# Seven half-size products for eight in the first layer of the last token block

## The chip, the cores and the metric

The kernel is one program on one core of a Trainium2 chip. The core's engines are named here as its profile names them: PE (TensorE, matrix products), with PEld for its weight loads; DVE (VectorE); ACT (ScalarE); POOL (GpSimd); SP (SyncE), which only issues transfers. Each engine takes its instructions in the order in which the program issued them to it, and instructions on different engines wait for each other through semaphores. The metric is the device time of one execution, in microseconds; before the change it was 321.52 us, the median of three runs (321.17 to 321.62).

## The reference

Two stages are chained. The first is a retention layer without softmax: for 8 batches and 8 heads of 576 positions with 64 columns, the scores q k^T / 8 are multiplied by a lower-triangular decay matrix gamma_h^(i-j), and then by v. Its output, as 4608 tokens of 512 columns, is the `x` of the second stage, a bilinear feed-forward layer with 1536 hidden columns:

```python
def _moe_ref(x, w_a, w_b, w_out):
    a = x @ w_a
    b = x @ w_b
    return (a * b @ w_out).astype(np.float32)
```

`a`, `b` and their product are here called the first layer (512 to 1536, twice), and the product with `w_out` the second (1536 to 512). The product of `a` and `b`, transposed, is `hT`: hidden columns on the partitions, tokens along the free axis.

## The kernel before

The 4608 tokens go through the feed-forward part in blocks: 512, 256, 256, and seven more of 512. In text and code they are counted by pairs of 256 tokens, `n` from 0 to 17 (`NP` is 18), so that the last block holds the pairs 16 and 17. The retention work of later tokens is threaded in between the products of earlier blocks. `ffn_block` is a generator that issues a few matrix products and yields their cost in units of one product of 512 columns; a list `todo` of (due time, function) pairs, written by hand, is worked off at those yields that are marked as an edge (in the first layer: after each hidden group's second half). A second list, `jobs`, holds small vector operations with a priority and a cost; `work(budget)` issues those that fit. The scheduler is manual: the order in which the Python code issues instructions is the order on each engine.

**First layer** (`ffn_block`, up to L1164). The 1536 hidden columns are 12 groups `F` of 128. For each group four products (one per 128 rows of `w_a`, 512 tokens wide) make `pa` in one PSUM bank, ACT copies it to `ha` in bfloat16 (L1152), four products make `pb` (L1159), and DVE multiplies `ha` by `pb` into `hT[:, F]` (L1164). `pa` and `pb` take turns in the four banks of the pool `ps_ffn` (tag `ab`); a bank is taken again when its reader is done, in the order in which banks came free.

**Second layer** (`rows_mixed`, L975 on). For the last six blocks it works on pairs of hidden groups (`p` from 0 to 5, groups `2p` and `2p+1`) and replaces eight products of half width by seven on sums of operands. The sums of weights (`wo_sums`) are made once. The sums of `hT` are made for each block by `row_sums` (L944): five additions or subtractions on DVE, three into `hsum` and two in place in `hT`. They are issued as jobs, for the pairs 0 to 3 together after group 7 and for the pairs 4 and 5 together after group 11. In the last block (`closing`), the products come in this order: ways 3 and 4 on `hT` as it is, way 1 on a sum, ways 5 and 2 on the two sums made in place, then 7 and 6 on sums. `lessen` and `add_last` (L1055, L1062) put the results together on DVE, and POOL adds two kept copies (L1045); the outputs of the block before last are stored from the list `formed`, in the last block.

The helper pools that matter below: `straight`, `crossed` and `less` (two buffers each, float32 copies of 128 x 512), `ps_sc` (two banks) and `ps_o` (one buffer of two banks), `stage` (the buffers of incoming q, k and v) and `nat`.

Of the kernel before, what the change touches and what calls it, by code (L numbers as in the profile page):

```python
# [18 lines left out]
def kernel(  # L19
# [10 lines left out]
    nc = tc.nc  # L30
# [4 lines left out]
    NTOK = B * S  # L35
    NC = DM // 128
# [8 lines left out]
    NP = NTOK // 256  # L45
# [34 lines left out]
    stage = pool("stage", 3)  # L80
    nat = pool("nat", 3)
# [5 lines left out]
    ha_pool = pool("ha", 6)  # L87
    o_pool = pool("osb", 4)
    late, early = {}, ExitStack()
# [13 lines left out]
    ps_ffn = pool("ps_ffn", 4, PS)  # L103
    opening, ps_sc, ps_o = ExitStack(), {}, {}
# [17 lines left out]
    wa_sb = big.tile([128, NC, DFF], BF16)  # L122
    wb_sb = big.tile([128, NC, DFF], BF16)
# [18 lines left out]
    shared = {}  # L142
# [117 lines left out]
    def pair_tables(step):  # L260
# [6 lines left out]
        else:  # L267
            for h in (2 * step - 2, 2 * step - 1):
# [660 lines left out]
    WIDE = DM // 2  # L929
# [11 lines left out]
        out = wo_sums[:, step // 3, p0:p0 + 2]  # L941
        nc.vector.tensor_tensor(out, one, other, op=op)

    def row_sums(hT, sums, p0, p1):  # L944

        even, odd = (hT[:, 2 * p0:2 * p1].rearrange(
            "p (f e) (g k s) -> p e k f g s", e=2, g=2, k=2)[:, e]
            for e in (0, 1))
        a11, a21, a12, a22 = even[:, 0], even[:, 1], odd[:, 0], odd[:, 1]
        to = [sums[:, i, p0:p1] for i in range(3)]  # L950
        return [(1, (p1 - p0) / 8 + 0.2,
                 lambda e=e: nc.vector.tensor_tensor(*e[:3], op=e[3]))  # L952
                for e in ((to[0], a11, a22, ALU.add),
                          (to[2], a12, a22, ALU.subtract),
                          (to[1], a21, a11, ALU.subtract),
                          (a12, a11, a12, ALU.add),
                          (a21, a21, a22, ALU.add))]

    def store_mixed(G, osb, cols=slice(0, 2 * DM), on=nc.sync):

# [17 lines left out]
    def store_formed():  # L978
        while formed:
            store_mixed(*formed.pop(0))  # L980

    def rows_mixed(tok0, hT, sums):
# [3 lines left out]
        pair = [tok0 // 256 + g for g in (0, 1)]  # L986
# [50 lines left out]
        crossed, lesses = {}, {}  # L1037
# [13 lines left out]
        def lessen(g):  # L1051
            lesses[g] = late["less"].tile([128, 2, WIDE], FP32, tag="less",
                                          name="less")
            for ks in (slice(0, 1), slice(1, 2)) if closing else (slice(0, 2),):
                nc.vector.tensor_tensor(  # L1055
                    lesses[g][:, ks],
                    both[g].unsqueeze(1).to_broadcast(
                        [128, ks.stop - ks.start, WIDE]),
                    crossed[g][:, ks], op=ALU.subtract)
# [33 lines left out]
        first, rest = range(NP2 - 1), (NP2 - 1,)  # L1093
# [19 lines left out]
        yield 0, True  # L1113

    def ffn_block(tb, tok0, n, runs):

        xT = x_of(tok0, n)
        hT = h_pool.tile([128, NF, 512], BF16, tag="h", name="hT")
        if tok0 >= 256 * MIXED:
            pools_mixed()  # L1120
            sums = late["hsum"].tile([128, 3, NF // 2, 2, 128], BF16, tag="hsum",
                                  name="hsum")
        f0 = 0
        for count in runs:
            has = {}
            if tb == 0 and f0 == 0:
                for c in range(2, NC):
                    for F in range(count):
                        begin_with(F, c, 1)
            for F in range(f0, f0 + count):  # L1130
                fs = slice(F * 128, (F + 1) * 128)
                pa = (begun[F] if tb == 0 and F in begun else
                      ps_ffn.tile([128, 512], FP32, tag="ab", name="pa"))
                for c in range(NC):
                    if tb == 0 and (F, 0, 0) in begun:
                        if (F, c, 1) not in begun:
                            begin_with(F, c, 1)
                        if c < NC - 1:
                            yield n / 512, False
                        continue  # L1140
                    nc.tensor.matmul(pa[:, 0:n], wa_sb[:, c, fs],  # L1141
                                     xT[:, c],
                                     start=(c == 0), stop=(c == NC - 1))
                    if c < NC - 1:
                        yield n / 512, False
                if n == 512 and tb:
                    pop()
                pass_on(1)
                if F == 2:
                    store_formed()  # L1150
                ha = ha_pool.tile([128, 512], BF16, tag="ha", name="ha")
                nc.scalar.copy(ha[:, 0:n], pa[:, 0:n])  # L1152
                has[F] = ha
                yield n / 512, False
            for F in range(f0, f0 + count):
                fs = slice(F * 128, (F + 1) * 128)
                pb = ps_ffn.tile([128, 512], FP32, tag="ab", name="pb")
                for c in range(NC):
                    nc.tensor.matmul(pb[:, 0:n], wb_sb[:, c, fs],  # L1159
                                     xT[:, c],  # L1160
                                     start=(c == 0), stop=(c == NC - 1))
# [12 lines left out]
                yield n / 512, True  # L1174
            f0 += count
        if tb == 0:
            yield from rows_together(tok0, hT, (0, 1))
        if tok0 >= 256 * MIXED:
            yield from rows_mixed(tok0, hT, sums)
            return  # L1180
        for u in range(2 if tb == 0 else 0, n // 128):
            osb = half_of(o_pool, u, [DM], FP32, "osb")
            po = ps_ffn.tile([128, 512], FP32, tag="ab", name="po")
            for F in range(NF):
                nc.tensor.matmul(po, hT[:, F, u * 128:(u + 1) * 128],  # L1185
                                 wo_sb[:, F],
                                 start=(F == 0), stop=(F == NF - 1))
# [12 lines left out]
            yield 1, True  # L1200
# [99 lines left out]
    starts, at = {}, 0.0  # L1300
# [84 lines left out]
        casts[n], turns[n] = placed[n] - 96, placed[n] - 58  # L1385
    for fn, places in ((ahead, casts), (turn, turns)):
        todo += [(at, fn, (n,)) for n, at in places.items()]
    todo.sort(key=lambda e: e[0])

    at = 0.0  # L1390
    tok = 0
    for tb, n in enumerate(blocks):
        runs = WCOLS if tb == 0 else [1] * NF
        for cost, edge in ffn_block(tb, tok, n, runs):
            at += cost
            while todo and edge and at >= todo[0][0]:
                _, fn, args = todo.pop(0)
# [33 lines left out]
```

## Time and profile before

| | |
|---|---|
| median of three runs | 321.52 us (321.17 to 321.62) |
| the profiled execution: its time / its span | 320.63 us / 318.4 us |
| PE busy | 308.0 us, 97% of the span |
| DVE / POOL / ACT busy | 198.9 / 155.6 / 145.7 us |
| last block, first layer (284.4 to 305.1 us) | PE 20.59, DVE 10.81, ACT 7.02, POOL 0.00 us busy of 20.70 |
| last block, second layer (305.1 to 314.5 us) | PE 9.38, DVE 5.55, ACT 2.40, POOL 2.51 us busy of 9.40 |
| from the last product to the end (314.5 to 318.4 us) | PE 0, DMA share 0.51 |

Times inside the execution are counted from the start of its span. In the lines of the timeline the columns are: start, length, engine, source line, operation, output <- inputs, shapes, number of instructions merged into the line, and in brackets the idle time before it with what ended it. The length of a merged line runs from its first start to its last end; a product's end is modelled and overlaps the next product, so the pace of products is read from start to start. In the lines of the groups, the numbers after the bar are busy time in total, mean ns of one, and the idle time before them.

### The profile page before, as it was taken

The numbers are of one execution on the slowest core, as the hardware profiler recorded it, in microseconds if no ns is written. First come the engines' busy times: TensorE is split into PE (matmuls) and PEld (weight loads), VectorE is DVE, ScalarE is ACT, GpSimd is POOL, SyncE is SP. The second block draws the span as 40 slices with busy tenths as digits, with TensorE's granted clock in tenths as the row PEclk, the third lists the DMA queues.
The fourth block names the chain that finished last, engine by engine and source line by source line (L and its number), as shares of the span: only waits on it lengthen the run. The fifth ranks groups of instructions, "written<-read, shape, count | busy, mean of one in ns | idle before, by whom it ended". The sixth has DMA issues, their size and how long they took to land.

```text
span 318.4 us, 9134 instructions
## 1 busy us (share of the span) xinstructions
PE 308.0 (97%) x3763; PEld 183.4 (58%) x3799; DVE 198.9 (62%) x376; ACT 145.7 (46%) x324; POOL 155.6 (49%) x169
## 2 busy tenths in 40 slices
PE   7899999999999999999999999999999999999995
PEld 3554457768544554448654864477446744674474
DVE  5745346867757563479658854776567656834563
ACT  7745346536435463454454534544434443423330
POOL 3990078664986577564796089506960300030003
PEclk9999999999999999999999999999999999999999
DMA  8999999999999999999999998974430110012004
GB/s 215 255 203 207 255 231 184 193 207 182 207 178 214 229 218 179 240 193 223 241 280 201 179 229 181 198 164 129 108 68 2 76 61 0 2 74 60 0 1 132
DMA packets 144793, 50.92 MB, mean 160 GB/s; under 512 B 126576, under 2 KB 141680, under 8 KB 144752
## 3 DMA queue, kind: packets, MB, share of 16 engines
q1 hardware_dynamic: 138272, 45.10, 70.9%
q0 software_dynamic: 5808, 4.72, 9.4%
q8 instruction: 29, 0.48, 0.6%
q10 hardware_dynamic: 672, 0.52, 0.5%
q14 instruction: 12, 0.10, 0.1%
HBM read 37.75 MB, written 9.44 MB: 148 GB/s over the span
## 4 chain that ended last, share of the span: by engine, by line
PE 90%; DVE 3%; DMA 2%; issue 2%; POOL 1%; SPq 1%; ACT 0%; DVEq 0%; POOLq 0%
PE pb L1159 29%; PE pa L1141 28%; PE m L1022 16%; PE po L1185 8%; DMA vf<-in_v_dram 2%; PE po L913 2%; PE sc L703 1%; PE o L731 1%; PE o L744 1%; SPq L175 1%; PE kv L632 1%; DVE hT L952 1%; POOL vb L365 1%; DVE sums L659 1%; PE pa L902 1%
## 5 line engine op out<-in xcount | busy, mean ns | idle before, releaser
L1164 DVE TENSOR_TENSOR hT<-ha,pb 128x512 bf16<-128x512 bf16 (+1 forms) x120 | 75.8, 632 | 80.4 <-PE pb L1159 68.5
L1159 PE MATMUL pb<-xT,wb_sb 128*128 128x512 bf16 (+1 forms) x478 | 111.5, 358 | 0.4
L1152 ACT CAST ha<-pa 128x512 bf16<-128x512 f32 (+1 forms) x120 | 64.9, 542 | 96.8 <-PE pa L1141 92.0
L1141 PE MATMUL pa<-xT,wa_sb 128*128 128x512 bf16 (+1 forms) x448 | 106.4, 356 | 1.9 <-issue 1.2
L1159 PEld LDWEIGHTS <-wb_sb 128*128 128x128 bf16 x480 | 46.8, 98 | 47.5 <-issue 1.9
L1141 PEld LDWEIGHTS <-wa_sb 128*128 128x128 bf16 x472 | 45.0, 98 | 43.0 <-DVE sums L659 0.2
L1045 POOL TENSOR_TENSOR osb<-crossed,straight 128x512 f32<-128x512 f32 x12 | 15.2, 1271 | 102.8 <-ACT crossed L1034 96.3
L589 POOL TENSOR_TENSOR vb<-vf,vs 128x1024 bf16<-128x1024 f32 (+1 forms) x17 | 29.6, 1743 | 4.5 <-PE pb L1159 1.7
L1022 PEld LDWEIGHTS <-hT 128*128 128x128 bf16 x288 | 28.1, 98 | 4.7 <-issue 0.3
L562 POOL TENSOR_TENSOR qkb<-qf,qs 64x1024 bf16<-64x1024 f32 x12 | 22.9, 1911 | 14.2 <-DMA qf<-in_q_dram 9.1
L1185 PE MATMUL po<-wo_sb,hT 128*128 128x512 bf16 x113 | 26.7, 379 | 0.8 <-issue 0.6
L1022 PE MATMUL m<-wo_sums,hsum 128*128 128x256 bf16 x216 | 25.7, 273 | 0.0
L567 POOL TENSOR_TENSOR qkb<-qf,qs 64x512 bf16<-64x512 f32 x24 | 24.8, 1052 | 0.7
L1022 PEld LDWEIGHTS <-hsum 128*128 128x128 bf16 x216 | 21.1, 98 | 2.4
L952 DVE TENSOR_TENSOR hsum<-hT 128x1024 bf16<-128x1024 bf16 (+1 forms) x36 | 20.3, 591 | 0.2
L578 POOL CAST qkb<-kf 64x1024 bf16<-64x1024 f32 (+1 forms) x17 | 15.9, 935 | 8.0 <-DMA kf<-in_k_dram 7.1
L712 DVE TENSOR_TENSOR sT<-sc,mask 128x512 bf16<-128x512 f32 x30 | 19.8, 680 | 0.0
L659 DVE TENSOR_TENSOR sums<-kv,sums 128x256 f32<-128x256 f32 x44 | 18.6, 422 | 1.4
L582 POOL CAST qkb<-kf 64x512 bf16<-64x512 f32 (+1 forms) x34 | 18.8, 581 | 0.9
L1185 PEld LDWEIGHTS <-hT 128*128 128x128 bf16 x120 | 11.2, 98 | 12.6
L1022 PE MATMUL m<-wo_sb,hT 128*128 128x256 bf16 x144 | 17.0, 273 | 0.1
L1022 PE MATMUL m<-wo_sums,hT 128*128 128x256 bf16 x144 | 16.9, 273 | 0.0
(111 smaller groups left out, 283.0 us busy)
## 6 DMA issues: line engine op xcount, KB each, us to landing
qf<-in_q_dram SPq DMA_DIRECT2D x32, 256.0 KB, 5.1
vf<-in_v_dram SPq DMA_DIRECT2D x32, 256.0 KB, 5.2
kf<-in_k_dram SPq DMA_DIRECT2D x31, 256.0 KB, 4.9
out_dram<-osb SPq DMA_DIRECT2D x9, 512.0 KB, 4.1
out_dram<-osb SPq DMA_DIRECT2D x22, 128.0 KB, 2.8
wo_sb<-in_moe_w_out_dram POOLq DMA_DIRECT2D x3, 512.0 KB, 16.0
out_dram<-osb SPq DMA_DIRECT2D x6, 256.0 KB, 4.2
qf<-in_q_dram SPq DMA_DIRECT2D x8, 128.0 KB, 4.2
```

The lines of the kernel that those rows point to most:

```text
L562: nc.gpsimd.tensor_tensor(per_head(qkb[0:64, Q]), per_head(t[0:64]), by[0:64].unsqueeze(2).to_broadcast([64, 2 * H, D]), op=ALU.mult)
L567: nc.gpsimd.tensor_tensor(per_head(qkb[64:128, Q])[:, 1 - r::2], per_head(t[64:128])[:, r::2], by[64:128, r::2].unsqueeze(2).to_broadcast( ...
L589: nc.gpsimd.tensor_tensor(vb[:, e].rearrange("p (h d) -> p h d", d=D), t[:, e].rearrange("p (h d) -> p h d", d=D), decay[:, at], op=ALU.mult)
L659: nc.vector.tensor_tensor(sums[:, i], own, prev, op=ALU.add)
L712: nc.vector.tensor_tensor(sT[:, on].rearrange("p c k s -> p (c k) s"), sc[on].rearrange("p c k s -> p (c k) s"), mask3.unsqueeze(1).to_bro ...
L952: lambda e=e: nc.vector.tensor_tensor(*e[:3], op=e[3]))
L1022: nc.tensor.matmul(to, rows, cols, start=(begins and p == 0), stop=True, skip_group_check=True)
L1141: nc.tensor.matmul(pa[:, 0:n], wa_sb[:, c, fs], xT[:, c], start=(c == 0), stop=(c == NC - 1))
L1152: nc.scalar.copy(ha[:, 0:n], pa[:, 0:n])
L1159: nc.tensor.matmul(pb[:, 0:n], wb_sb[:, c, fs], xT[:, c], start=(c == 0), stop=(c == NC - 1))
L1164: nc.vector.tensor_tensor(hT[:, F, 0:n], has[F][:, 0:n], pb[:, 0:n], op=ALU.mult)
L1185: nc.tensor.matmul(po, hT[:, F, u * 128:(u + 1) * 128], wo_sb[:, F], start=(F == 0), stop=(F == NF - 1))
```

## The change

Three things change, all for the last block of 512 tokens.

1. Its first layer goes through a new generator, `last_layer`. For four of the six pairs of hidden groups (`SEVENS`: 0, 1, 3, 4) the product of [2 x 128 hidden columns, 512] by [512, 512 tokens], cut in two along each axis, is made from seven products of half size instead of eight, for `w_a` and `w_b` alike (`m` is 0 and 1, side by side in one bank): 28 matrix products of 256 columns for a pair in place of 16 of 512 columns. Partial results accumulate in the banks `main` (ways 1, 6, 7, 4), `side` (5, 3) and `aside` (2). Three of them are copied out by ACT on the way (`keep`); three quarters of a pair's `hT` are made by a DVE addition of bank and copy and a POOL multiplication (`gated`), and the fourth by ACT and DVE as before. The pairs 2 and 5 keep the old way ("a" and "b" in `ORDER`).
2. The operands need sums. `combine` makes four sums of weights for a pair of hidden-group pairs and a matrix (two pairs at a time, `combos`, in buffers of `stage`): 12 instructions on POOL and 4 on DVE, due in the block before last. `combine_rows` makes four sums of `x` of the last block on DVE, issued in `rows_mixed` of the block before last, between `lessen` and `add_last`.
3. `row_sums` for the last block is issued for each pair alone: 30 DVE instructions on 256 columns in place of 5 on 1024 and 5 on 512. The first of a pair's five comes ahead of other jobs (0.9). The budget for jobs after each step of `ORDER` is `SHARE`.

```diff
-    def row_sums(hT, sums, p0, p1):
+    def row_sums(hT, sums, p0, p1, shared=0):
...
+        order = (2, 0, 1, 3, 4)
...
+        return [(0.9 if i == 2 and p1 == p0 + 1 else 1, (p1 - p0) / 8 + 0.2,
+                 lambda e=ways[i]: nc.vector.tensor_tensor(*e[:3], op=e[3]))
+                for i in order if i >= shared]
...
             lessen(g)
+        if pair[1] == NP - 3:
+            for i in range(4):
+                combine_rows(i)
...
+    def combine(p, m, i):
...
+        out, one, other, op = [(s3, a11, a21, ALU.subtract),
+                               (s1, a21, a22, ALU.add),
+                               (s2, a22, s3, ALU.subtract),
+                               (s4, a12, s2, ALU.subtract)][i]
+        (nc.vector if i == 3 else nc.gpsimd).tensor_tensor(
+            out, one, other, op=op)
...
+    def combine_rows(i):
...
+        out, one, other, op = [(t1, b12, b11, ALU.subtract),
+                               (t3, b22, b12, ALU.subtract),
+                               (t2, b11, t3, ALU.add),
+                               (t4, b21, t2, ALU.subtract)][i]
+        nc.vector.tensor_tensor(out, one, other, op=op)
...
+        def quarter(p, way):
...
+            to = st["aside" if way == 2 else
+                    "side" if way in (3, 5) else "main"]
...
+                w, x = {1: (a11, xT[:, 0:2, g0]), 2: (a12, xT[:, 2:4, g0]),
+                        3: (s4, xT[:, 2:4, g1]), 4: (a22, t4), 5: (s1, t1),
+                        6: (s2, t2), 7: (s3, t3)}[way]
+                for c in (0, 1):
+                    nc.tensor.matmul(to[:, m], w[:, c], x[:, c],
...
+        def keep(name, own):
+            t = late[name].tile([128, 2, WIDE], FP32, tag=name, name=name)
+            nc.scalar.copy(t, own)
+            return t
+
+        def gated(t, own, to):
+            nc.vector.tensor_tensor(t, own, t, op=ALU.add)
+            nc.gpsimd.tensor_tensor(to, t[:, 0], t[:, 1], op=ALU.mult)
+
+        def after(p, way):
...
+            if way == 1:
+                st["first"] = keep("straight", st["main"])
+            elif way == 5:
+                st["third"] = keep("less", st["side"])
+            elif way == 6:
+                st["second"] = keep("crossed", st["main"])
+            elif way == 2:
+                gated(st["first"], st["aside"], hT[:, F0, g0])
+            elif way == 3:
+                gated(st["second"], st["side"], hT[:, F0, g1])
+            elif way == 7:
+                gated(st["third"], st["main"], hT[:, F1, g1])
+            else:
+                ha = ha_pool.tile([128, 512], BF16, tag="ha", name="ha")
+                nc.scalar.copy(ha[:, g0], st["main"][:, 0])
+                nc.vector.tensor_tensor(hT[:, F1, g0], ha[:, g0],
+                                        st["main"][:, 1], op=ALU.mult)
...
+    ORDER = ((1, 0), (5, 0), (2, 0), (6, 0), (1, 1), (3, 0), (7, 0), (5, 1),
+             (2, 1), (6, 1), (4, 0), ("a", 4), (3, 1), (7, 1), ("b", 4),
+             ("a", 5), (4, 1), ("b", 5),
+             (1, 3), (5, 3), (2, 3), (6, 3), (1, 4), (3, 3), (7, 3), (5, 4),
+             (2, 4), (6, 4), (4, 3), ("a", 10), (3, 4), (7, 4), ("b", 10),
+             ("a", 11), (4, 4), ("b", 11))
+    SHARE = {1: 0, 5: 0, 2: 0, 6: 0.4, 3: 0, 7: 0.4, 4: 0, "a": 0.4, "b": 0.7}
...
+            if done is not None:
+                jobs.extend(row_sums(hT, sums, done, done + 1, SHARED))
+            work(SHARE[way])
+        work(math.inf, 1)
...
+        if tok0 == NTOK - 512:
+            yield from last_layer(xT, hT, sums)
+            yield from rows_mixed(tok0, hT, sums)
+            return
...
+    todo += [(starts[NP - 4] + 2 + 4.2 * i, combine,
+              (SEVENS[i // 8 * 2], i // 4 % 2, i % 4)) for i in range(16)]
```

More of the change, by code (lines that the diff above doesn't have):

```diff
@@ L950, in row_sums @@
         to = [sums[:, i, p0:p1] for i in range(3)]
[L951 to L957, printed above, removed]
+        ways = ((to[2], a12, a22, ALU.subtract),
+                (to[1], a21, a11, ALU.subtract),
+                (to[0], a11, a22, ALU.add),
+                (a12, a11, a12, ALU.add),
+                (a21, a21, a22, ALU.add))
+        order = (2, 0, 1, 3, 4)
+        for i in range(shared):
+            out, one, other, op = ways[i]
+            nc.gpsimd.tensor_tensor(out, one, other, op=op)
+        return [(0.9 if i == 2 and p1 == p0 + 1 else 1, (p1 - p0) / 8 + 0.2,
+                 lambda e=ways[i]: nc.vector.tensor_tensor(*e[:3], op=e[3]))
+                for i in order if i >= shared]
     def store_mixed(G, osb, cols=slice(0, 2 * DM), on=nc.sync):
@@ L1113, in rows_mixed, with quarter_weights @@
         yield 0, True
+    SEVENS = (0, 1, 3, 4)
+    SHARED = 0
+    combos = {}
+    def quarter_weights(m, p0, count=1):
+        w = (wa_sb, wb_sb)[m][:, :, 256 * p0:256 * (p0 + count)].rearrange(
+            "p c (q e f) -> p e c q f", e=2, f=128)
+        return [[w[:, e, c:c + 2] for c in (0, 2)] for e in (0, 1)]
+    def combine(p, m, i):
+        if (p, m) not in combos:
+            combos[p, m] = stage.tile([128, 4, 2, 2, 128], BF16,
+                                      tag=("qf", "kf")[m], name="combo")
+            combos[p + 1, m] = combos[p, m]
+        (a11, a12), (a21, a22) = quarter_weights(m, p, 2)
+        s3, s1, s2, s4 = (combos[p, m][:, k] for k in range(4))
+        out, one, other, op = [(s3, a11, a21, ALU.subtract),
[4 more added lines that the diff above has]
+            out, one, other, op=op)
@@ new lines @@
+    row_combos = []
+    def combine_rows(i):
+        if not row_combos:
+            row_combos.append(nat.tile([128, 4, 2, 256], BF16, tag="qkb",
+                                       name="rows"))
+        x = x_of(256 * (NP - 2), 512)
+        (b11, b12), (b21, b22) = [[x[:, c:c + 2, 256 * g:256 * g + 256]
+                                   for g in (0, 1)] for c in (0, 2)]
+        t1, t3, t2, t4 = (row_combos[0][:, k] for k in range(4))
+        out, one, other, op = [(t1, b12, b11, ALU.subtract),
[3 more added lines that the diff above has]
+        nc.vector.tensor_tensor(out, one, other, op=op)
@@ new lines, in layer_mixed @@
+    def layer_mixed(xT, hT):
+        t1, t3, t2, t4 = (row_combos[0][:, k] for k in range(4))
+        g0, g1 = slice(0, 256), slice(256, 512)
+        state = {}
+        def quarter(p, way):
+            if way == 1:
+                state[p] = {
+                    "main": ps_ffn.tile([128, 2, 256], FP32, tag="ab",
+                                        name="lm"),
+                    "side": ps_sc[0].tile([128, 2, 256], FP32, tag="sc",
+                                          name="ls")}
+            st = state[p]
+            if way == 2:
+                st["aside"] = ps_o[0].tile([128, 2, 2, 256], FP32, tag="o",
+                                           name="la")[:, 0]
+            to = st["aside" if way == 2 else
+                    "side" if way in (3, 5) else "main"]
+            for m in (0, 1):
+                (a11, a12), (_, a22) = (
+                    [t[:, :, 0] for t in ts] for ts in quarter_weights(m, p))
+                s3, s1, s2, s4 = (combos[p, m][:, k, :, SEVENS.index(p) % 2]
+                                  for k in range(4))
+                w, x = {1: (a11, xT[:, 0:2, g0]), 2: (a12, xT[:, 2:4, g0]),
[3 more added lines that the diff above has]
+                    nc.tensor.matmul(to[:, m], w[:, c], x[:, c],
+                                     start=(way in (1, 2, 5) and m == c == 0),
+                                     stop=True, skip_group_check=True)
+                    yield 0.5, False
+        def keep(name, own):
[6 more added lines that the diff above has]
+        def after(p, way):
+            st = state[p]
+            F0, F1 = 2 * p, 2 * p + 1
+            if way == 1:
+                st["first"] = keep("straight", st["main"])
[14 more added lines that the diff above has]
+                                        st["main"][:, 1], op=ALU.mult)
+        return quarter, after
@@ new lines, with last_layer @@
+    ORDER = ((1, 0), (5, 0), (2, 0), (6, 0), (1, 1), (3, 0), (7, 0), (5, 1),
[5 more added lines that the diff above has]
+    SHARE = {1: 0, 5: 0, 2: 0, 6: 0.4, 3: 0, 7: 0.4, 4: 0, "a": 0.4, "b": 0.7}
+    def last_layer(xT, hT, sums):
+        quarter, after = layer_mixed(xT, hT)
+        has = {}
+        for i, (way, at) in enumerate(ORDER):
+            done = None
+            if way in ("a", "b"):
+                F = at
+                p1 = ps_ffn.tile([128, 512], FP32, tag="ab", name="p" + way)
+                for c in range(NC):
+                    w = wa_sb if way == "a" else wb_sb
+                    nc.tensor.matmul(p1, w[:, c, F * 128:F * 128 + 128],
+                                     xT[:, c], start=(c == 0),
+                                     stop=(c == NC - 1))
+                    yield 1, False
+                if way == "a":
+                    has[F] = ha_pool.tile([128, 512], BF16, tag="ha",
+                                          name="ha")
+                    nc.scalar.copy(has[F], p1)
+                else:
+                    nc.vector.tensor_tensor(hT[:, F], has[F], p1, op=ALU.mult)
+                    if F % 2:
+                        done = F // 2
+            else:
+                yield from quarter(at, way)
+                after(at, way)
+                if way == 4:
+                    done = at
+            if i == 3:
+                store_formed()
+            if done is not None:
+                jobs.extend(row_sums(hT, sums, done, done + 1, SHARED))
+            work(SHARE[way])
+        work(math.inf, 1)
```

## The prediction

> **What bounds the kernel now.** I read the page's busy shares and chain first, then the windows of the last two blocks, then the timelines of PE, DVE and POOL around the last block, and last the groups of POOL and DVE by shape for prices.
>
> ```profile
> PE 308.0 (97%) x3763; PEld 183.4 (58%) x3799; DVE 198.9 (62%) x376; ACT 145.7 (46%) x324; POOL 155.6 (49%) x169
> ...
> PE 90%; DVE 3%; DMA 2%; issue 2%; POOL 1%; SPq 1%; ACT 0%; DVEq 0%; POOLq 0%
> ```
>
> PE is busy 97% of the span, and 90% of the chain that ended last is PE.
>
> ```profile
> 252.70:284.40 31.70, 31.49 (x337) 18.95 (x340) 19.68 (x38) 11.66 (x24) 2.54 (x2) 1.00 0.09 34
> 284.40:305.10 20.70, 20.59 (x96) 9.39 (x97) 10.81 (x17) 7.02 (x12) 0.00 (x0) 1.00 0.16 52
> ```
>
> Columns: stretch, length, then busy us and instructions of PE, PEld, DVE, ACT and POOL, and the granted clock. The second row is the layer that changes: PE has no gap in it, DVE is busy 52%, POOL not at all, and the clock is 1.00. So what is taken from PE here is time, as long as the other engines keep up.
>
> ```profile
> 279.18 2.78 PE L1022 MATMUL m<-wo_sb,hT 128*128 128x256 bf16 x24
> ...
> 285.29 1.03 PE L1159 MATMUL pb<-xT,wb_sb 128*128 128x512 bf16 x4
> 286.15 1.03 PE L1141 MATMUL pa<-xT,wa_sb 128*128 128x512 bf16 x4
> ...
> 305.14 2.35 PE L1022 MATMUL m<-wo_sums,hT 128*128 128x256 bf16 x20
> 307.33 0.82 PE L1022 MATMUL m<-wo_sums,hsum 128*128 128x256 bf16 x6
> ```
>
> Start to start, 92 wide products take 305.14 - 285.29 = 19.85 us, 0.2158 each; 20 half-wide ones take 307.33 - 305.14 = 2.19 us, 0.109 each (0.1092 over longer stretches). A half-wide product costs 51% of a wide one.
>
> ```profile
> 281.36 2.58 POOL L1045 TENSOR_TENSOR osb<-crossed,straight 128x512 f32<-128x512 f32 x2 [29.20 <-ACT crossed L1034]
> ...
> 282.62 0.69 DVE L1055 TENSOR_TENSOR less<-m,crossed 128x512 f32<-128x512 f32 x1 [0.62 <-ACT crossed L1034]
> 283.37 0.75 DVE L1062 TENSOR_TENSOR osb<-m,less 128x256 f32<-128x256 f32 x2
> ...
> 306.62 1.09 DVE L952 TENSOR_TENSOR hsum<-hT 128x512 bf16<-128x512 bf16 x3
> 307.63 0.75 DVE L952 TENSOR_TENSOR hT<-hT 128x512 bf16<-128x512 bf16 x2
> ```
>
> These rows give the paces of DVE: three sums of 512 in 307.63 - 306.62 = 1.01 us, 0.337 each; sums of 1024 start 0.60 apart (306.02, 306.62). The slope is 0.267 per 512, so 0.07 is fixed, and a sum of 256 comes to 0.204. That is an estimate; no row has one.
>
> ```profile
> 170.37 1.90 POOL L589 TENSOR_TENSOR vb<-vf,vs 128x1024 bf16<-128x1024 f32 x1
> ...
> 170.87 1.95 DVE L952 TENSOR_TENSOR hsum<-hT 128x1024 bf16<-128x1024 bf16 x1
> ```
>
> A DVE sum of two SBUF operands, usually 0.69, takes 1.95 when issued 0.5 us into a POOL instruction of 1.90: it ends 0.55 after POOL does (172.27, 172.82). It waits for the running POOL instruction. DVE instructions with a PSUM operand (L1164, L712) keep 0.68 to 0.69 beside the same POOL work.
>
> **The change, part by part.** Times continue those of the profiled execution.
>
> *Products.* A changed pair issues 28 half-wide products for 16 wide ones: 28 x 0.1092 = 3.06 for 16 x 0.2158 = 3.45, 0.395 less. Four pairs: **-1.58**. The bounds: the pace of L1022, or, if these products ran at 3.45/28 = 0.123, no gain at all. I take L1022's: same width, same weight size.
>
> *Sums of weights.* POOL, 12 on 512 columns. No POOL row has bfloat16 inputs; the nearest are 128x512 f32 at 1271 ns and vb 128x512 at 1086. Their operands are weights loaded long before, so POOL takes them up at 252.2, when its adds of the block before end (249.58 + 2.58), and is done by 265.3 to 267.4, ahead of the first DVE sum of that block (268.57). Cost nothing, the cover being POOL's empty queue from 252.2 to 281.36. The four on DVE take 0.34 each and may wait up to 1.27 for a running POOL instruction; the fourth of a set follows its POOL operand by an edge or more. Behind them on DVE wait the products into hT, whose banks are asked for again some 2.6 us after they were filled, against 0.27 + 0.69 for reading them. Nothing on PE; 0 to 0.3 if the wait falls into the busy stretch at 261 to 264.
>
> *Sums of x.* Four on DVE after 283.31 (282.62 + 0.69). The first waits for POOL's second add, 281.36 + 2.58 = 283.94; the second follows at 0.34; the third reads the second and the fourth the third, 0.47 each (0.41 + 0.06, as 282.62 to 283.37 shows for 0.69). They end at 285.5. Queued behind are the four `add_last`, 0.34 each: the first two end at 286.28 instead of 284.12, the others at 286.96. They free the buffers of `less`, into which (5,0) is copied by ACT: 286.33 to 286.91. Way 3 of pair 0 needs that copy; PE comes to it at 284.42 + 5 x 0.437 = 286.60 and starts at 286.97 (waits of PE on ACT ended 0.05 to 0.06 after it early in the trace: ACT qkT to PE sc at 11.37, 11.43). **+0.37**, and 0.06 more for way 7 behind a late `crossed`. Without the POOL collision, or with it doubled, 0.1 to 0.9.
>
> *Elementwise work of the layer.* Per changed pair DVE has three additions from PSUM (0.61 start to start, as L1164 before L952) and one half (0.34), four pairs 8.7; two old pairs 4 x 0.61 = 2.4; ACT three copies of 0.58 and one half; POOL three multiplications of 256. The price of the last: 722 ns (128x256 f32, L462) and 615 (128x256 from f32 into bf16, L365); 0.72 is nearest, two full float32 operands. Upper bound 1.27, the 512 row. At 0.72 the pairs' chains hold: way 6 needs way 1's copy, 0.20 + 0.58 + 0.06 after it, and comes 0.87 after; way 4 needs way 7's addition and comes at least 1.3 us after.
>
> *Sums of hT.* 30 x 0.204 = 6.1 for what took 10 (5 x 0.60 and 5 x 0.337, 4.7). `SHARE` lets 15 out before group 11's product, 7 in the first half of `ORDER` and 8 in the second. Each may wait for a running POOL multiplication, at most 0.72; I count seven such waits, 1.4 us. DVE then has 40 instructions, 15.6 us, in the 19.6 us of the layer: it keeps up, by 4 us.
>
> *The end of the layer.* PE is done at 305.14 - 1.58 + 0.43 = 304.0. Group 11's product starts on DVE at 304.27 (0.27 after, as in every group before) and the remaining 15 sums follow from 304.88. The second layer asks last for the in-place sum a12 of pair 5, the 14th: 304.88 + 14 x 0.204 + 0.05 = 307.8. PE wants it after 20 + 6 + 4 + 5 = 35 half-wide products, 304.0 + 3.82 = 307.8. Before, the same sum was there 0.9 us early (308.04 for 308.97). So the cover is gone, and what is late next is this sum: **+0.02** at 0.204. At 0.25 a sum it is 0.9, at 0.28 1.5; at a POOL multiplication of 0.8, 0.4, and at 0.9, 0.8 (DVE then falls behind). This is the forecast's weak place.
>
> *Rest.* The stores of block 7 leave a step earlier or later on SP, with 25 us to spare; no transfer is added. The tail from 314.5 on is untouched.
>
> Sum: -1.58 + 0.43 + 0.02 = -1.1, with 0 for the weights. Profiled time 320.63 - 1.1 = 319.5. That execution stands 0.9 under the median of 321.52, so I put the median at 321.52 - 1.05 = **320.5**.
>
> [...]
>
> **The rivals.**
>
> *The small sums cost their length, not their pace (slower, or even).* Lengths are 0.69 at 1024 and 0.41 at 512, so 0.28 at 256. If each waits for the one before to end (a semaphore between them would do it), 14 take 3.9 us and a12 of pair 5 is 1.5 us late: -1.1 + 1.5 = +0.4, 321.9. It decides from 0.26 on. Against it: L952 of 512 runs three in a row at its pace. For it: no row has 256 columns, and in-place sums follow sums of the same columns. [...]
>
> *POOL is the pace of the layer.* Twelve multiplications at 1.0 us or more hold `straight`, `crossed` and `less`, hold up sums, and with them DVE: at 1.0 way 4 waits and the end comes 0.8 later than before, 322.3; at 0.9 it is -0.3, 321.2. Against it: 722 ns measured; for it, the lock with DVE, which lengthened vb from 1.90 to 2.22 at 144.7.
>
> *A bank.* If the bank that "b" 5 or "b" 11 takes is the one that (4,1) or (4,4) has just filled, PE waits for ACT and DVE: 0.2 + 0.38 + 0.05 + 0.42 + 0.06, some 1.2 each: 321.7 for one, 322.7 for both. Banks are given out in the order in which they come free, and then another one is free earlier.
>
> *The weights are not hidden.* Were POOL's sums over 1.9 us each, they would run past 275 into block 7's DVE sums and their wait of up to 1.9; some +1, 322. Against it, 1086 and 1271.
>
> *No gain in the products.* At 0.123 the change is +0.1: 321.6.
>
> **How the numbers follow.** A measurement of this kernel can tell about 0.2%, 0.64 us, from no change. The forecast (320.0 to 320.9) has 0.60. Part of its end lost (a sum at 0.23 to 0.25, or POOL at 0.8 to 0.9: 320.8 to 321.4) has 0.15, a third of which is still faster by over 0.2%. The sums at their length has 0.10, half of it same and half slower; POOL as the pace 0.05, a bank 0.04, the weights 0.04, all slower; no gain in the products 0.02, same. Faster 0.65, same 0.17, slower 0.18. Range: 319.9 is the whole cut of PE with no wait; above, to leave out only the doubled bank and POOL beyond 1.0, 322.2.
>
> **What would show it.** PE's layer ends about 1.1 us earlier against its start, with one gap of 0.4 at way 3 of pair 0 and 112 half-wide products at 0.109. DVE's sums of 256 start 0.2 apart. POOL has 12 sums between 252 and 268 and 12 multiplications of about 0.72 in the last layer. In the second layer PE waits for DVE at way 5 by 0.1 or less; a wait of a microsecond there, or a PE gap before "b" 5, "b" 11 or (4,4), makes the prediction wrong, and so does any gap in block 7.

## The result and the profile after

The changed kernel takes 319.18 us (median of 6; 318.93 to 319.87), against 321.54 us (6; 321.17 to 321.62) for the kernel before on the same chip: a ratio of 0.9932, 95% interval 0.9919 to 0.9945. It is faster by 2.36 us, where 1.05 was forecast, and the time lies 0.7 us below the lower end of the range. The profiled execution of the changed kernel takes 319.40 us, span 317.7.

The page of the changed kernel, first the busy time of each engine, then the chain that ended last by engine:

```profile
PE 310.2 (98%) x3847; PEld 188.2 (59%) x3847; DVE 208.3 (66%) x412; ACT 149.1 (47%) x332; POOL 177.8 (56%) x193
...
PE 88%; DVE 5%; SPq 2%; DMA 2%; issue 1%; ACT 1%; DVEq 0%; ACTq 0%
```

PE still bounds the kernel. Its busy time only seems to grow from 308.0 us: the page of before lacks 36 of the products (3763 records), and three more traces of that kernel have 3799 and 311.4 to 311.9 us. DVE has 9.4 us more to do and POOL 22.2. The windows of the changed kernel show where (stretch, length, busy us and instructions of PE, PEld, DVE, ACT, POOL, then granted clock, DMA share, GB/s): block 7's second layer, the last block's first layer, the last block's second layer up to its final 18 products.

```profile
275.80:284.95 9.15, 9.15 (x85) 8.21 (x84) 5.30 (x12) 2.25 (x4) 2.54 (x2) 1.00 0.00 0
284.95:304.42 19.47, 19.39 (x146) 14.07 (x145) 16.98 (x41) 10.18 (x20) 8.68 (x12) 1.00 0.17 55
304.42:311.63 7.21, 7.21 (x68) 6.42 (x67) 5.37 (x21) 1.82 (x4) 1.27 (x1) 1.00 0.01 3
```

In the layer that changed DVE is now busy 16.98 of 19.47 us, 87%, where it was 52%, and PE still has hardly a gap. The timeline of PE in the changed kernel, around the only two waits and at the start of the second layer:

```profile
286.95 0.38 PE L1192 MATMUL lm<-xT,wb_sb 128*128 128x256 bf16 x2
287.41 0.60 PE L1192 MATMUL ls<-xT,combo 128*128 128x256 bf16 x4
287.90 0.60 PE L1192 MATMUL lm<-rows,combo 128*128 128x256 bf16 x4
...
304.42 2.35 PE L1027 MATMUL m<-wo_sums,hT 128*128 128x256 bf16 x20
```

Two products from 286.95 on last 0.22, so PE could have gone on at 287.17 and did at 287.41: a wait of 0.24. The four after it take 0.437, to 287.85; the next start at 287.90, 0.05 later. After that PE runs without a gap.

Three marks lead through every trace: the start of block 7's second layer, the start of the last block's second layer, and the start of its final 18 products.

| kernel | block 7's second layer | last block's second layer | between them | final 18 products | from there to the span's end |
|---|---|---|---|---|---|
| before | 275.25 | 305.14 | 29.89 | 312.35 | 6.04 |
| changed | 275.80 | 304.42 | 28.62 | 311.63 | 6.06 |

The first mark differs from one execution to the next: it lay between 275.4 and 276.0 in three more executions of before. The 0.55 is there before the sums of weights begin: the start of block 6's second layer lies 31.78 us ahead of the mark in both (243.47 and 244.02), and POOL's first sum starts at 252.67. It is counted as chance here; over all traces the mark lies between 275.2 and 276.0 in before and between 275.4 and 277.3 in the changed kernel and its variants, and no run shows whether that is chance alone. The stretch between the first two, 1.27 us shorter, is what the change did in the last block; I had forecast 1.15 for it (1.58 less 0.43). The profiled pair adds up: 320.63 - 1.27 + 0.55 (chance) + 0.02 (tail) - 0.53 (time outside the span, 2.23 before and 1.70 after) = 319.40. But the medians are 2.36 apart: the profiled execution of before stands 0.9 below its median, that of the changed kernel 0.22 above. So another microsecond had to be found in executions that these two traces don't show.

### The profile page after: what moved, and what is told of

The parts are those of the page before. It is cut to its first block, busy times and chain, and to the rows that moved or that the text cites. A ratio compares the mean times of both kernels' runs of the same rounds, so it can differ in the third digit from the quotient of the medians.

```text
span 317.7 us, 9344 instructions
## 1 busy us (share of the span) xinstructions
PE 310.2 (98%) x3847; PEld 188.2 (59%) x3847; DVE 208.3 (66%) x412; ACT 149.1 (47%) x332; POOL 177.8 (56%) x193
## 4 chain that ended last, share of the span: by engine, by line
PE 88%; DVE 5%; SPq 2%; DMA 2%; issue 1%; ACT 1%; DVEq 0%; ACTq 0%
PE pb L1320 26%; PE pa L1302 25%; PE m L1027 15%; PE po L1346 8%; PE lm L1192 2%; SPq L175 2%; DMA qf<-in_q_dram 2%; PE po L913 2%; PE sc L703 1%; PE o L744 1%; PE o L731 1%; PE kv L632 1%; DVE hT L961 1%; PE pb L1248 1%; PE pa L1248 1%
## 5 line engine op out<-in xcount | busy, mean ns | idle before, releaser
L1325 DVE TENSOR_TENSOR hT<-ha,pb 128x512 bf16<-128x512 bf16 (+1 forms) x108 | 67.6, 626 | 68.7 <-PE pb L1320 58.4
L1320 PE MATMUL pb<-xT,wb_sb 128*128 128x512 bf16 (+1 forms) x432 | 99.3, 355 | 0.1
L1302 PE MATMUL pa<-xT,wa_sb 128*128 128x512 bf16 (+1 forms) x424 | 97.6, 355 | 0.1
L1313 ACT CAST ha<-pa 128x512 bf16<-128x512 f32 (+1 forms) x108 | 58.0, 538 | 81.8 <-PE pa L1302 79.2
L1320 PEld LDWEIGHTS <-wb_sb 128*128 128x128 bf16 x432 | 42.1, 98 | 41.9 <-issue 1.9
L1302 PEld LDWEIGHTS <-wa_sb 128*128 128x128 bf16 x424 | 40.3, 98 | 37.9 <-issue 0.4
L1346 PE MATMUL po<-wo_sb,hT 128*128 128x512 bf16 x120 | 27.8, 379 | 0.0
L961 DVE TENSOR_TENSOR hsum<-hT 128x256 bf16<-128x256 bf16 (+2 forms) x48 | 22.4, 494 | 0.4
```

The source lines that it names most:

```text
L961: lambda e=ways[i]: nc.vector.tensor_tensor(*e[:3], op=e[3]))
L1302: nc.tensor.matmul(pa[:, 0:n], wa_sb[:, c, fs], xT[:, c], start=(c == 0), stop=(c == NC - 1))
L1320: nc.tensor.matmul(pb[:, 0:n], wb_sb[:, c, fs], xT[:, c], start=(c == 0), stop=(c == NC - 1))
L1325: nc.vector.tensor_tensor(hT[:, F, 0:n], has[F][:, 0:n], pb[:, 0:n], op=ALU.mult)
L1346: nc.tensor.matmul(po, hT[:, F, u * 128:(u + 1) * 128], wo_sb[:, F], start=(F == 0), stop=(F == NF - 1))
```

## The experiments

**First set: is the excess chance, and does each part do what it should?** The changed kernel again, unaltered:

> The changed kernel once more, beside the kernel before on the same chip. Theory A (all of the gain is made in the last block, where the two traces differ by 1.3 us; the rest of the 2.4 us lies between single executions): 1.0 to 1.6 us less than before. Theory B (about 1.1 us come from outside the last block, and with this program every time): 2.1 to 2.6 us less again, and the spans of the runs, or the time outside the spans, differ by more than the last block does.

Measured: 319.50 us (6 runs) against 321.38 (17), ratio 0.9943 (0.9923 to 0.9962). The stretch is 28.63. The gain of 1.88 lies between the ranges of the two theories, and its interval (1.2 to 2.5) just reaches the 1.26 of the stretch. So some 0.6 us of excess came back, and it isn't in the stretch; that it is more than chance, these runs alone do not show.

Only the sums of weights and of x, with the last block as it was before:

```
         if tok0 == NTOK - 512:
-            yield from last_layer(xT, hT, sums)
-            yield from rows_mixed(tok0, hT, sums)
-            return
+            pass
```

> The sums of weights and of x are made where the changed kernel makes them, but the last block's first layer and its row sums are done the old way (the sums are not used). Theory A: 0 to 0.4 us slower than before, the late add_last holding a bank at the start of the last block. Theory B, with the cause in what the program adds ahead of the last block: about 1 us faster than before.

The prepared sums are made and not used. Measured: 321.33 us (12 runs), ratio 1.0002 (0.9987 to 1.0018), stretch 29.92. Twenty additional instructions on POOL and DVE cost nothing that can be seen, and they give nothing either.

The sums of x ahead of the two `cross` and `lessen`:

```
         work(math.inf)
         pass_on(math.inf)
+        if pair[1] == NP - 3:
+            for i in range(4):
+                combine_rows(i)
         for g in (0, 1):
             yield from cross(g)
             lessen(g)
-        if pair[1] == NP - 3:
-            for i in range(4):
-                combine_rows(i)
```

> The changed kernel with the four sums of x issued ahead of the products 5 and 2 of the block before last, where DVE stands idle for 3.2 us and POOL has nothing, instead of behind the second lessen. The prediction's account of the start of the layer (0.43 us of waits behind late sums): the gaps of PE at way 3 and way 7 of pair 0 go, 0.4 us less than the changed kernel. Rival (those waits only move to the next late copy): no difference beyond 0.15.

Measured: 319.21 us (5 runs), ratio 0.993 (0.991 to 0.995), stretch 303.75 - 275.40 = 28.35. The timeline of PE in this kernel, at the same two places:

```profile
286.55 0.38 PE L1192 MATMUL lm<-xT,wb_sb 128*128 128x256 bf16 x2
286.77 0.60 PE L1192 MATMUL ls<-xT,combo 128*128 128x256 bf16 x4
287.22 0.60 PE L1192 MATMUL lm<-rows,combo 128*128 128x256 bf16 x4
...
303.75 2.35 PE L1027 MATMUL m<-wo_sums,hT 128*128 128x256 bf16 x20
```

Way 3 follows after 0.22 and way 7 after 0.45: both waits are gone, and with them 0.27 of the stretch, where 0.4 was expected. It is 1.54 shorter than before, against a full cut of 1.58. By its trace this is the best of the kernels, by 0.27 us; the times (319.21 and 319.50 on one chip) don't separate it from the changed kernel.

Two pairs instead of four:

```
-             (1, 3), (5, 3), (2, 3), (6, 3), (1, 4), (3, 3), (7, 3), (5, 4),
...
+             ("a", 6), ("b", 6), ("a", 7), ("b", 7), ("a", 8), ("b", 8),
+             ("a", 9), ("b", 9), ("a", 10), ("b", 10), ("a", 11), ("b", 11))
```

> The pairs 0 and 1 by seven products as in the change, the pairs 3, 4 and 5 the old way; all sums are made. Theory A: half of the cut of 1.58 less the waits of 0.43 at its start, 0.3 to 0.5 us less than before. Theory B with a fixed 1.1 us: 1.3 to 1.6 us less.

Measured: 319.77 us (6 runs), ratio 0.9954 (0.9936 to 0.9973), stretch 305.00 - 275.60 = 29.40, 0.49 less than before. The stretch went as forecast for half the change, and again the time fell by more, 1.6 us. So the excess doesn't grow with the number of pairs.

**Second set: where is the excess?** Before three more times and the changed kernel once, all traced.

> The kernel before, traced again, to see where an ordinary execution of it (321.4 us) is longer than the one that was profiled first (320.6 us). From the start of the second layer of the block before last to the start of the last block's second layer it took 29.89 us there (28.62 with the change), and 275.25 us up to that point. Theory A (what is left of the difference lies in the waits for inputs of the first 275 us, by chance of the execution): 29.9 us again, and a start of 275.2 to 277. Theory C (long runs of wide products at the end draw a lower clock, and the change breaks them up): 30.3 us or more, with a granted clock below 1.00 there.

> The kernel before once more. Theory A: 29.9 us for that stretch and a start anywhere from 275.2 to 277; theory C: 30.3 us or more with a clock below 1.00.

> The kernel before a third time. Theory A: 29.9 us for that stretch and a start anywhere from 275.2 to 277; theory C: 30.3 us or more with a clock below 1.00.

> The changed kernel traced again beside them. Theory A: 28.6 us for the stretch, and a start of 275.2 to 277 as with the kernel before. Theory C: 28.6 us and a clock of 1.00, the start no different from that of the kernel before.

Measured: before 321.15, 320.99 and 321.56 us (8 runs each), ratios 1.0, 1.0016 and 1.0016, each interval holding 1; changed 319.09 (8 runs), 0.9935 (0.9908 to 0.9961). The stretch is 29.89 in all three traces of before and 28.62 in that of the changed kernel. Theory A falls, since the starts (275.4 to 276.0 in before, 275.9 in the changed kernel) do not favour the changed kernel. Theory C falls too: the windows of the first trace have the clock at 1.00 through the stretch and beyond, up to the last product.

```profile
275.37:305.26 29.89, 29.89 (x181) 17.59 (x180) 15.78 (x29) 9.26 (x16) 2.54 (x2) 1.00 0.11 36
305.26:314.60 9.34, 9.34 (x85) 8.13 (x83) 5.56 (x14) 2.40 (x5) 2.49 (x2) 1.00 0.10 24
314.60:317.00 2.40, 0.00 (x0) 0.00 (x0) 0.42 (x1) 0.00 (x0) 0.06 (x1) 1.00 0.90 261
317.00:319.20 2.20, 0.00 (x0) 0.00 (x0) 0.00 (x0) 0.00 (x0) 0.00 (x0) 0.52 0.28 99
```

The difference is in what comes after the products. From the final 18 products to the end, two of these traces of before take 6.8 and 6.9 us (319.3 - 312.47 in the first) and one 6.1; every trace of the changed kernel and its variants above takes 6.0 to 6.1. The transfers in the stretch from 311 to 316 us, first in the profiled execution of before that the prediction read (6.04 from the final products to the end), then in the first of the three, with its final products ahead. The rows of queues give packets, MB and the share of the 16 engines; those of stores give their number, the size of each and the median us from issue to landing.

```profile
DMA packets 404, 0.79 MB, mean 159 GB/s; under 512 B 80, under 2 KB 208, under 8 KB 404
...
q1 hardware_dynamic: 336, 0.66, 48.4%
q10 hardware_dynamic: 68, 0.14, 7.3%
...
out_dram<-osb SPq DMA_DIRECT2D x6, 128.0 KB, 2.2
out_dram<-osb ACTq DMA_DIRECT2D x1, 256.0 KB, 2.3
```

```profile
312.47 2.13 PE L1022 MATMUL m<-wo_sums,hsum 128*128 128x256 bf16 x18
...
DMA packets 184, 0.53 MB, mean 107 GB/s; under 512 B 54, under 2 KB 54, under 8 KB 183
...
q1 hardware_dynamic: 177, 0.50, 42.0%
q8 instruction: 1, 0.02, 1.2%
q10 hardware_dynamic: 6, 0.01, 0.9%
...
out_dram<-osb SPq DMA_DIRECT2D x6, 128.0 KB, 2.6
out_dram<-osb ACTq DMA_DIRECT2D x1, 256.0 KB, 3.0
```

q1 and q10 carry the last stores. In the second execution one packet of instructions (q8, 16 KB) lies among them, at 312.5 us, and in the same five microseconds 0.53 MB are moved instead of 0.79; a store of 128 KB lands after a median of 2.6 us instead of 2.2. In the first, the same packet comes after the span's end, and the stretch from 318.4 to 320 us holds nothing else:

```profile
q8 instruction: 1, 0.02, 5.2%
```

In that execution 2.23 us lie outside the span instead of 1.7. So before seems to pay in either case, once inside the span and once behind it. In the changed kernel the packet starts at 306.8 us, ahead of the last stores:

```profile
DMA packets 2, 0.02 MB, mean 7 GB/s; under 512 B 0, under 2 KB 0, under 8 KB 0
...
q8 instruction: 1, 0.02, 1.7%
q14 instruction: 1, 0.01, 0.8%
```

That is the stretch from 306 to 309.5 us. Counted from the start of the final 18 products, the packet lies 4.8 us ahead with the whole change, 2.5 with half of it (309.7 us) and at their start in the first of the three traces of before: steps of 2.3 and 2.5 us, some 21 and 23 half-wide products of 0.109, and 24 products are what each half of the change adds to TensorE's instructions. This suggests that q8 feeds TensorE, and that the change moved the fetch only by making TensorE's program longer.

**Third set: move the fetch and nothing else.** A product of 512 columns is made as two of 256, in the first layers of blocks 4 to 6, far ahead of the last block. That adds instructions to TensorE and no columns:

```
+    TWICE = [(NTOK - 512 * k, F) for k in (5, 4, 3)
+             for F in range(12)][:12]
...
-                    nc.tensor.matmul(pa[:, 0:n], wa_sb[:, c, fs],
-                                     xT[:, c],
-                                     start=(c == 0), stop=(c == NC - 1))
+                    for at in ((slice(0, 256), slice(256, 512))
+                               if (tok0, F) in TWICE else (slice(0, n),)):
+                        nc.tensor.matmul(pa[:, at], wa_sb[:, c, fs],
+                                         xT[:, c, at],
+                                         start=(c == at.start == 0),
+                                         stop=(c == NC - 1),
+                                         skip_group_check=True)
```

With 12 groups of four products that is 48 more, in before. The changed kernel got 20 groups (80 more) and 32 (128 more), and before 32 as well.

> The kernel before, with 48 products of block 4's first layer each made as two of 256 columns: the same columns, 96 more instructions on TensorE's queue (as many as the change adds), nothing altered in the last two blocks. Theory D (an instruction fetch of queue 8 that falls among the last stores in many executions of before is the part of the gain that the last block does not show): the last fetch moves from some 312.5 us of the span to about 307, the time from the last product group's x18 row to the end is 6.1 us and no longer 6.8, the stretch from block 7's second layer to the last one's stays 29.89, and the median falls by 0.4 to 0.9 us against before. Theory E (the tail's 0.8 us is chance, or comes from the last block's own work): the median stays within 0.3 us of before, and the tail is as often 6.8 as before.

> The changed kernel, with 80 products of the first layers of blocks 4 and 5 made in two halves: TensorE's queue is 256 instructions longer than before's, so that a fetch of 256 instructions falls where before has it. Theory D: the last fetch is at about 312 us, amid the stores, the tail is 6.8 us in many executions, and the median is 0.4 to 0.9 us above the changed kernel (319.6 to 320.3 us, a ratio of 0.995 to 0.997 to before). Theory E: within 0.3 us of the changed kernel's 319.2 (ratio 0.9935).

> The changed kernel with 128 products in two halves: 256 instructions more than the changed kernel, so that the last fetch is where the changed kernel has it, about 307 us. It carries still more split products than the run with 80. Theory D: tail 6.1 us, median within 0.3 us of the changed kernel's (ratio about 0.9935 to before), below the run with 80 by 0.4 to 0.9. If the split products themselves cost, this run is slower than the one with 80. Theory E: all the same within 0.3.

> The kernel before with 128 products in two halves: 256 instructions more, so that the last fetch is where before has it. Theory D: no gain, the median within 0.3 us of before, and slower than the run of before with 48 by 0.4 to 0.9. Theory E, or a gain that comes from halving products: as fast as the run with 48 or faster.

All on one chip, 12 runs each, against 321.30 us for before (35 runs):

| kernel | products added | us | ratio (95%) | stretch | last q8 packet at | final 18 products to the end |
|---|---|---|---|---|---|---|
| before | 48 | 320.56 | 0.9972 (0.9948 to 0.9997) | 29.89 | 308.6 | 6.05 |
| before | 128 | 321.65 | 1.0006 (0.9986 to 1.0026) | 29.89 | after the end | 6.04 |
| changed | 80 | 320.20 | 0.9966 (0.9945 to 0.9987) | 28.62 | 313.2 | 7.14 |
| changed | 128 | 319.44 | 0.9937 (0.9916 to 0.9958) | 28.62 | 306.8 | 6.05 |

Before with 48 more products: its final products, the instruction packet (306 to 309.5 us), and the stores from 311 to 316 us:

```profile
312.32 2.13 PE L1022 MATMUL m<-wo_sums,hsum 128*128 128x256 bf16 x18
...
q8 instruction: 1, 0.02, 1.7%
...
out_dram<-osb SPq DMA_DIRECT2D x6, 128.0 KB, 2.2
out_dram<-osb ACTq DMA_DIRECT2D x1, 256.0 KB, 2.3
```

The window of the changed kernel with 80 more products, then its final products and its transfers from 311 to 316 us:

```profile
277.31:305.93 28.62, 28.44 (x227) 22.27 (x228) 22.30 (x52) 12.43 (x24) 11.20 (x14) 1.00 0.12 38
```

```profile
313.14 2.13 PE L1027 MATMUL m<-wo_sums,hsum 128*128 128x256 bf16 x18
...
q8 instruction: 1, 0.02, 1.4%
...
out_dram<-osb SPq DMA_DIRECT2D x5, 128.0 KB, 3.1
out_dram<-osb ACTq DMA_DIRECT2D x1, 256.0 KB, 3.1
```

Its last block is as quick as the changed kernel's, and its stores land late: 3.1 us instead of 2.2 and 2.3. (This traced execution is the slowest of its twelve, 322.0 us, because its first mark lies at 277.31 too.) Theory D had the direction of all four outcomes, in time and in the trace, and theory E falls. D's sizes were missed in places: the packet of before with 48 more lies at 308.6 us and not at 307, the tail of the changed kernel with 80 more is 7.1 us and not 6.8, and before with 128 more is 0.35 slower than before (at most 0.3 was expected) and 1.09 slower than with 48 (0.4 to 0.9). Before gains 0.74 us (interval 0.1 to 1.7) from 48 products split in two, which adds no columns, and the changed kernel loses 0.76 (320.20 against 319.44) when the fetch is put back. A further 128 products bring the fetch back to its place and make one packet more, 31 for 30. So it is TensorE's program that is fetched, about 128 products with their weight loads at a time. The sums alone fit this: they add nothing to that program, and its last packet came behind the end of the span.

The time outside the span says the same over many runs. In the kernels whose fetch falls late (before in all its runs of these three sets, with and without 128 more products, the sums alone, and the changed kernel with 80 more) it is over 1.85 us in 26 of 139 runs; in the others (the changed kernel, with 128 more, with the sums of x early, with half the change, and before with 48 more) in none of 55. In the four traces with the packet behind the end it is 1.9 to 2.55, in all others 1.66 to 1.76. Those 26 runs also have shorter spans than the other runs of their kernel in seven of eight groups (318.8 against 319.65 us in the largest, the 35 runs of before, at the same time of 321.3), as if the fetch were paid for either inside the span or behind it.

What is open: whether the late fetch falls among the stores or behind the end differs from one execution of the same kernel to the next, and no run tells what decides it. Nor is it shown how one packet of 16 KB slows stores of 1 MB; the runs show only that it does.

## Why the prediction was wrong, by its steps

**Products, -1.58: right.** Without the two waits the stretch is 1.54 shorter, and the rival of no gain in the products falls.

**Sums of weights, 0: right.** The timeline of POOL in the changed kernel, its first and last sums and its first multiplication:

```profile
252.67 2.27 POOL L1145 TENSOR_TENSOR combo<-wa_sb 128x512 bf16<-128x512 bf16 x2
...
265.28 1.15 POOL L1145 TENSOR_TENSOR combo<-wb_sb,combo 128x512 bf16<-128x512 bf16 x1
...
288.02 0.73 POOL L1204 TENSOR_TENSOR hT<-straight 128x256 bf16<-128x256 f32 x1 [3.54 <-DVE straight L1203]
```

The sums take 1.15 each in the mean (266.43 - 252.67 = 13.76 for twelve) and are over at 266.4, inside the bounds (265.3 to 267.4). PE lost nothing to them, since block 6's second layer starts 31.78 us ahead of block 7's before and after. The rival in which the weights are not hidden falls, with POOL idle until 281.90.

**Sums of x, +0.43: the mechanism right, the size 0.14 too large.** The timeline of DVE in the changed kernel:

```profile
283.77 1.32 DVE L1162 TENSOR_TENSOR rows<-xT 128x512 bf16<-128x512 bf16 x2
285.13 0.88 DVE L1162 TENSOR_TENSOR rows<-xT,rows 128x512 bf16<-128x512 bf16 x2
285.93 1.41 DVE L1067 TENSOR_TENSOR osb<-m,less 128x256 f32<-128x256 f32 x4
...
307.05 0.48 DVE L961 TENSOR_TENSOR hT<-hT 128x256 bf16<-128x256 bf16 x2
307.45 0.48 DVE L961 TENSOR_TENSOR hsum<-hT 128x256 bf16<-128x256 bf16 x2
307.85 0.48 DVE L961 TENSOR_TENSOR hT<-hT 128x256 bf16<-128x256 bf16 x2
```

The sums of x push back `add_last` as foreseen, and PE waits 0.24 and 0.05 at the two places named, 0.29 in all. Moving them ahead of `lessen` took both waits away.

**Elementwise work: right.** POOL's multiplications take 0.72 to 0.78 each, mostly 0.73 (0.72 taken), and the rival of POOL as the pace falls with DVE at 87% and PE without a gap; so does the one of a bank, since no gap stands before `"b"` 5 or `"b"` 11.

**Sums of hT: right, at the weak place.** Two of them start every 0.40 us, so 0.20 each against 0.204, while each alone is 0.28 long. The in-place sum a12 of pair 5 is the first of the row at 307.85 and ends at 308.13; PE comes to it at 304.42 + 3.82 = 308.24, 0.1 later. The rival that charges their length falls.

**The tail, and the step from the profiled execution to the median: wrong.** "The tail from 314.5 on is untouched" and "That execution stands 0.9 under the median of 321.52, so I put the median at 321.52 - 1.05" took the tail and the 0.9 for constants that the change would leave alone. They were not: the changed kernel's profiled execution stands 0.22 above its median. Part of both was the late fetch of TensorE's instructions, which the profiled execution of before shows in one of its two forms (behind the end of the span, with 2.23 us outside the span), and the lateness goes with the change because TensorE's program becomes longer by 48 products. The prediction had put this term at nothing; measured by itself it is -0.74 us (-0.1 to -1.7). With the stretch's -1.27 that makes -2.0, inside the interval of the first comparison (-1.8 to -2.6). Between before and the changed kernel with 128 more, on one chip, it is 1.86: 0.74 for the place of the fetch and 1.12, the rest, for the last block. That the profiled execution came out at 319.40, where 319.5 was forecast, is partly luck: the start 0.55 later and the 0.53 less outside the span cancel. (The sum of the terms is -1.13; that -1.05 was carried to the median matters little beside this.) The range held bounds for everything that the change does in the last block and none for where its instructions put the rest of the program.

## What to carry to other kernels

Where instructions are added to or taken from an engine (here TensorE, with 16 KB to a packet), ask also where its instruction fetches fall afterwards, above all whether one is among the last stores (with one there, the end came 0.7 to 1.1 us later here); the packets of the instruction queues stand in the trace with their times, those behind the end of the span too. When a small change gives more or less than its own stretch of the trace shows, pad the engine's program with instructions that do no additional work, once by a part of a fetch and once by a whole one (here 48 and 128 products with their weight loads): this tells the place of the code from the change itself. And a profiled execution that lies away from the median should be explained before its sum is carried over to the median.

## What the runs showed of the hardware that was not expected

- TensorE's program is fetched in packets of 16 KB, about one per 128 products with their weight loads (0.49 MB in 30 packets for the 3847 products of the changed kernel; 31 packets with 128 more). In the traces with one of them among the last 1 MB of stores, the end came 0.7 to 1.1 us later (6.8 to 7.1 us from the final products to the end, instead of 6.05).
- DVE's sums of 256 bfloat16 columns, both operands in SBUF, start 0.20 us apart in the row from 307.05 to 308.33 us of the changed kernel, while each takes 0.28.
- In the first of the three traces of before the granted clock of TensorE is 0.52 in the window from 317.0 us above, the last product being over at 314.6. In the execution that the prediction read it is still 1.00 from 317.0 us to the end of the span at 318.4. The mean clock (0.997 for the first of the three traces of before, 1.000 for the one that the prediction read) therefore told nothing of the products; half the change has 0.997 too, with 6.06 us from its final products to the end.
